# Sliding-window attention before a GeGLU layer: one 256-query score product for key block 2 in place of two 128-query ones, from batch 3 on

One core of one Trainium2 chip. The metric is device time in microseconds (us) of one execution; lower is better.

## The reference

```python
# q, k, v: (8 batches, 8 heads, 576 tokens, 64)
scores = (q @ k^T) / 8 + bias          # bias = -slope(head) * |i - j|
mask   = (i - j >= 0) & (i - j < 128)  # a window of 128 keys, causal
attn   = softmax(where(mask, scores, -1e9))
x      = (attn @ v) as (4608 tokens, 512)
out    = (gelu(x @ w_gate) * (x @ w_val)) @ w_out      # 512 -> 1536 -> 512
```

## The kernel before

The tokens of a batch are shifted by 64 and cut into five blocks of 128, so that the first half of block 0 is padding. With a window of 128, keys of block j meet queries of blocks j and j+1 only. Two heads are worked on as a pair (`i` = 0, 1), each in its own 64 rows of the matmul array; `c` counts the four pairs. Scores are computed with keys on the partitions, so the exponential on ACT and a multiplication by a constant mask and bias on DVE (`emask`: 128 columns for the block's own queries, 128 for the next block's) give the probabilities without a transposition.

The queries come in part 0 (tokens 0 to 319) and part 1 (320 to 575). A score product has one column for each of its queries, and every group of products fills banks of 512 columns of PSUM. The program keeps eight such banks; part 1 of batch 3 takes all eight (four pairs, two banks each):

```python
PART = ((0, 320), (320, 576))
# key block, first and last query of the part that it serves
PIECES = (((0, 0, 192), (1, 64, 320), (2, 192, 320)),
          ((2, 0, 128), (3, 0, 256), (4, 128, 256)))
PCOL = ({0: 64, 1: 256}, {4: 0, 2: 128, 3: 256})

def score(b, c, i, j, qj, n, ps, col):        # keys of block j, n query blocks from qj
    nc.tensor.matmul(out=ps[:, col:col + 128 * n]..., lhsT=blocks(kT, b, i, c, j, 1)...,
                     rhs=blocks(qT, b, i, c, qj, n), start=True, stop=True)

def scores2(b, later=None):                   # the small piece: block 2 with its own queries
    ...
    for c in range(4):
        for i in (0, 1):
            score(b, c, i, 2, 2, 1, ps[i], 128 * c)
    ...                                       # exponential, mask

def scores(b, s, cs, then=None, later=None):
    for c in cs:
        ps = [bank(), bank()]
        for j, qj, n, col in (((0, 0, 2, 0), (1, 1, 2, 256)),
                              ((4, 4, 1, 0), (2, 3, 1, 128), (3, 3, 2, 256)))[s]:
            for i in (0, 1):
                score(b, c, i, j, qj, n, ps[i], col)
    ...                                       # exponential; mask now, or in the list `later`

def sums(b, s):                               # softmax denominators
    for j, a, e in PIECES[s]:                 # key blocks in this order
        for i in (0, 1):
            for c in range(4):
                nc.tensor.matmul(..., lhsT=ones..., rhs=prob(b, s, c, i, j, e - a), ...)
    ...                                       # reciprocal
```

The stages overlap: while the feed-forward layer of token group g runs on TensorE, the scores of batch g+2 and the sums and value products of batch g+1 are put in between. In the loop over g the sums stand here:

```python
        for f in range(7 if g == 0 else 0, NF):
            gate_val(g, f)                    # 8 matmuls of 512 columns, 1.73 us
            ...
            if 2 <= g < B - 1:
                if f == (1 if g == 2 else 0):
                    sums(g + 1, 0)
                if f == (2 if g == 2 else 0):
                    sums(g + 1, 1)
```

So batch 3 (g = 2) has its two sums behind columns 1 and 2 of gate and value; batches 4 to 7 have both behind column 0.

The softmax here doesn't subtract the row's maximum and nothing guards it: scores larger than these inputs give would overflow.

Of the kernel before, what the change touches and what calls it, by code (L numbers as in the profile page):

```python
# [19 lines left out]
          ((2, 0, 128), (3, 0, 256), (4, 128, 256)))  # L20


PCOL = ({0: 64, 1: 256}, {4: 0, 2: 128, 3: 256})


@with_exitstack
def kernel(
# [39 lines left out]
    def bank():  # L67
        ps = psum.tile([128, 512], FP32, name="ps")
        for _ in range(heat.pop()):
            nc.tensor.matmul(out=ps, lhsT=zeros[:, 0:128], rhs=zeros, start=True, stop=True)  # L70
        heat.append(0)
        return ps
# [98 lines left out]
    def blocks(t, b, i, c, j, n):  # L171
        if b < 2:
            return by_pair(t[b])[64 * i:64 * i + 64, c, 128 * j:128 * (j + n)].rearrange(
                "p (n t) -> p n t", n=n)
        return t[b % 2][64 * i:64 * i + 64, j:j + n, c, :]
# [7 lines left out]
    probs, probs2 = {}, {}  # L183

    def score(b, c, i, j, qj, n, ps, col):
        nc.tensor.matmul(  # L186
            out=ps[:, col:col + 128 * n].rearrange("p (n t) -> p n t", n=n),
            lhsT=blocks(kT, b, i, c, j, 1).rearrange("p n t -> p (n t)"),
            rhs=blocks(qT, b, i, c, qj, n),
            start=True, stop=True)  # L190

    def exp(dst, src):
        nc.scalar.activation(out=dst, in_=src, func=AF.Exp, scale=0.125)  # L193

    def mask(dst, m):
        nc.vector.tensor_tensor(out=dst, in0=dst, in1=m, op=ALU.mult)  # L196

    def scores2(b, later=None):

        P = p2_pool.tile([128, 4, 2, 128], BF16, name="P2")  # L200
        probs2[b] = P
        ps = [bank(), bank()]
        for c in range(4):
            for i in (0, 1):
                score(b, c, i, 2, 2, 1, ps[i], 128 * c)
        for i in (0, 1):
            exp(P[:, :, i, :], ps[i].rearrange("p (c n) -> p c n", c=4))
        if later is None:
            for i in (0, 1):
                mask(P[:, :, i, :], emask[:, i:8:2, 0:128])  # L210
        else:
            later.append((P.rearrange("p c i n -> p (c i) n"), emask[:, :, 0:128]))

    def scores(b, s, cs, then=None, later=None):


        pss = []
        for c in cs:
            ps = [bank(), bank()]
            pss.append(ps)  # L220
            for j, qj, n, col in (((0, 0, 2, 0), (1, 1, 2, 256)),
                                  ((4, 4, 1, 0), (2, 3, 1, 128), (3, 3, 2, 256)))[s]:
                for i in (0, 1):
                    score(b, c, i, j, qj, n, ps[i], col)
        if then:
            then()
        for c, ps in zip(cs, pss):
            P = p_pool[s].tile([128, 2, 512], BF16, name="P")
            probs[b, s, c] = P
            for i in (0, 1):  # L230
                exp(P[:, i, :], ps[i])
            args = (P.rearrange("p i (n x) -> p i n x", n=2),
                    emask[:, 2 * c:2 * c + 2, :].unsqueeze(2).to_broadcast((128, 2, 2, 256)))
            if later is None:
                mask(*args)
            else:
                later.append(args)

    def prob(b, s, c, i, j, n):
        if (s, j) == (0, 2):  # L240
            return probs2[b][:, c, i, 0:n]
        return probs[b, s, c][:, i, PCOL[s][j]:PCOL[s][j] + n]

    sumrow, recip = {}, {}

# [12 lines left out]
    def sums0(s):  # L258
        w = WIDE[s]
        ps = bank()  # L260
        todo = []
        for c in range(4):
            for i in (0, 1):
                for j, a, e in ((0, 0, 192), (1, 64, 320)) if s == 0 else PIECES[1]:
                    todo.append((c, i, j, a, e))
        if s == 0:
            todo += [(c, i, 2, 192, 320) for i in (0, 1) for c in range(4)]
        mms = []
        for c, i, j, a, e in todo:
            for x in range(a // w, (e + w - 1) // w):  # L270
                lo, hi = max(a, w * x), min(e, w * x + w)
                g = x if s == 0 else 2 * x + c // 2
                h = 2 * c + i
                mms.append((g, ones4[:, min(j, 1), 32 * h:32 * h + 32] if s == 0 else
                            ones8[:, 32 * (h % 4):32 * (h % 4) + 32],
                            prob(0, s, c, i, j, e - a)[:, lo - a:hi - a], lo - w * x, hi - w * x))
        for n, (g, lhsT, rhs, lo, hi) in enumerate(mms):
            nc.tensor.matmul(
                out=ps[32 * g:32 * g + 32, lo:hi], lhsT=lhsT, rhs=rhs,
                start=all(m[0] != g for m in mms[:n]), stop=all(m[0] != g for m in mms[n + 1:]),  # L280
                skip_group_check=True)
        nc.vector.reciprocal(row(0)[:, PART[s][0]:PART[s][0] + w], ps[:, 0:w])
# [19 lines left out]
    def sums(b, s):  # L302

        ps = bank()
        for j, a, e in PIECES[s]:
            for i in (0, 1):
                for c in range(4):
                    nc.tensor.matmul(  # L308
                        out=ps[32 * c:32 * c + 32, a:e],
                        lhsT=ones[:, min(j, 1), i, :], rhs=prob(b, s, c, i, j, e - a),  # L310
                        start=(i == 0 and j == 2 * s), stop=(i == 1 and j == 2 * s + 2),
                        skip_group_check=True)
        lo, hi = PART[s]
        nc.vector.reciprocal(row(b)[:, lo:hi], ps[:, 0:hi - lo])  # L314
# [27 lines left out]
    def values(b, s, cs=range(4)):  # L342
        lo, hi = PART[s]
        pss = []
        for c in cs:
            ps = bank()
            pss.append(ps)
            for j, a, e in PIECES[s]:
                for i in (0, 1):
                    h = 2 * c + i  # L350
                    nc.tensor.matmul(  # L351
                        out=ps[64 * i:64 * i + 64, a:e],
                        lhsT=vb[b % 2][:, j, 64 * h:64 * h + 64],
                        rhs=prob(b, s, c, i, j, e - a),
                        start=(j == 2 * s), stop=(j == 2 * s + 2), skip_group_check=True)
        for c, ps in zip(cs, pss):
            nc.vector.tensor_tensor(  # L357
                out=xT[:, c, b * S + lo:b * S + hi], in0=ps[:, 0:hi - lo],
                in1=recip[b][:, c, lo:hi], op=ALU.mult)
# [126 lines left out]
    first((0, 1))  # L486
    keep_busy(5)
    scores(0, 0, (0, 1), lambda: (keep_busy(2), first((2,)), first((3,))))
    keep_busy(1)
    scores(0, 0, (2, 3))  # L490
    scores2(0)
    keep_busy(4)
    rest((0, 1))
    rest((2, 3))
    keep_busy(3)
    sums0(0)
    masks, tails = [], []
    scores(0, 1, (0,), None, masks)
    keep_busy(2)
    spread0(0, (act, dve, act, dve))  # L500
# [56 lines left out]
    def flush():  # L557
        for args in masks:
            mask(*args)
        masks.clear()  # L560

    RUN = {"s2": scores2, "s": scores, "sum": sums, "spread": spread_pe, "pv": values,
           "masks": flush, "transposes": transposes_dma, "last": out_last}

# [72 lines left out]
```

## Time and profile before

| | |
|---|---|
| median of the first 3 runs | 358.26 us (358.25 to 358.6) |
| TensorE (PE) busy | 350.5 us, 98% |
| PE's share of the chain that ended last | 89% |
| VectorE (DVE), ScalarE (ACT) busy | 53%, 52% |
| PE's waits, all of the run | 2.9 us, none listed after 100 us |

The prediction below shows the lines and reads them. The early part of a run, loads above all, varies from run to run. So I use the chain in order of time (start, length, what, count), which is the work that led to the last instruction, followed back step by step. From it I take a stretch that begins with the first gate product after batch 3's scores and ends at the start of the last output products. In the kernel before:

```profile
107.69 3.61 PE ps L370 x16
111.30 0.61 PE ps L308 x24
111.91 1.83 PE ps L370 x8
113.74 0.56 PE ps L308 x24
...
351.13 2.63 PE ps L407 x24
```

The stretch is 351.13-107.69 = 243.44 us. The two x24 groups are batch 3's sums of part 0 and part 1.

### The profile page before, as it was taken

The numbers are of one execution on the slowest core, as the hardware profiler recorded it, in microseconds if no ns is written. First come the engines' busy times: TensorE is split into PE (matmuls) and PEld (weight loads), VectorE is DVE, ScalarE is ACT, GpSimd is POOL, SyncE is SP. The second block draws the span as 40 slices with busy tenths as digits, with TensorE's granted clock in tenths as the row PEclk, the third lists the DMA queues.
The fourth block names the chain that finished last, engine by engine and source line by source line (L and its number), as shares of the span: only waits on it lengthen the run. The fifth ranks groups of instructions, "written<-read, shape, count | busy, mean of one in ns | idle before, by whom it ended". The sixth has DMA issues, their size and how long they took to land.

```text
span 357.3 us, 7072 instructions
## 1 busy us (share of the span) xinstructions
PE 350.5 (98%) x2855; PEld 175.0 (49%) x2855; DVE 188.4 (53%) x327; ACT 185.8 (52%) x342; POOL 103.3 (29%) x137
## 2 busy tenths in 40 slices
PE   8999999999999999999999999999999999999996
PEld 3568555444454445445454545445444444444443
DVE  5677469434888646656546554745474403403320
ACT  5874496536878366632973287337833133313322
POOL 8843569600940094002910192004000000000000
PEclk9999999999999999999999999999999999999999
DMA  8999999999999199683998499759205020011002
GB/s 93 177 195 197 203 146 200 147 157 167 134 155 180 39 176 177 120 171 61 145 187 173 90 131 203 139 128 93 85 11 132 26 94 1 2 60 57 2 29 88
DMA packets 145888, 42.62 MB, mean 119 GB/s; under 512 B 131608, under 2 KB 138776, under 8 KB 145856
## 3 DMA queue, kind: packets, MB, share of 16 engines
q0 software_dynamic: 106624, 18.88, 69.7%
q1 hardware_dynamic: 36432, 17.31, 21.7%
q10 hardware_dynamic: 2800, 5.99, 7.7%
q8 instruction: 22, 0.36, 0.4%
q14 instruction: 10, 0.08, 0.1%
HBM read 43.65 MB, written 9.53 MB: 149 GB/s over the span
## 4 chain that ended last, share of the span: by engine, by line
PE 89%; DVE 3%; DMA 3%; POOL 3%; issue 1%; ACT 0%; POOLq 0%; ACTq 0%; DVEq 0%
PE ps L370 52%; PE ps L393 25%; PE ps L351 4%; PE ps L186 4%; DMA wv<-in_moe_w_val_dram 3%; PE ps L308 2%; DVE P L196 1%; DVE r L314 1%; PE ps L407 1%; POOL vb L99 1%; POOL vb L123 0%; POOL wg L133 0%; PE ps L334 0%; POOL ks L123 0%; DVE kT L157 0%
## 5 line engine op out<-in xcount | busy, mean ns | idle before, releaser
L377 DVE TENSOR_TENSOR hT<-ps,gelu 128x512 bf16<-128x512 f32 (+2 forms) x115 | 74.3, 654 | 107.6 <-PE ps L370 92.6
L376 ACT ACTIVATE gelu<-ps 128x512 bf16<-128x512 f32 (+2 forms) x115 | 65.1, 571 | 116.1 <-PE ps L370 114.9
L370 PE MATMUL ps<-xT,wg 128*128 128x512 bf16 (+2 forms) x460 | 112.3, 366 | 0.1
L370 PE MATMUL ps<-xT,wv 128*128 128x512 bf16 (+2 forms) x460 | 112.1, 366 | 0.1
L393 PE MATMUL ps<-wo,hT 128*128 128x512 bf16 x420 | 95.8, 380 | 0.0
L193 ACT ACTIVATE P<-ps 128x512 bf16<-128x512 f32 x144 | 73.1, 631 | 7.6 <-PE ps L186 7.5
L370 PEld LDWEIGHTS <-wv 128*128 128x128 bf16 x460 | 44.6, 98 | 49.1 <-DMA wv<-in_moe_w_val_dram 0.4
L370 PEld LDWEIGHTS <-wg 128*128 128x128 bf16 x460 | 43.2, 98 | 47.1 <-issue 0.3
L196 DVE TENSOR_TENSOR P<-P,emask 128x1024 bf16<-128x1024 bf16 (+1 forms) x79 | 48.8, 640 | 30.9 <-ACT P L193 30.5
L393 PEld LDWEIGHTS <-hT 128*128 128x128 bf16 x420 | 38.9, 98 | 47.7 <-issue 3.6
L99 POOL DMA_DIRECT2D vb<-in_v_dram x40 | 33.9, 879 | 12.9 <-DMA ks<-in_k_dram 5.3
L398 ACT COPY osb<-ps 128x512 f32<-128x512 f32 x31 | 18.7, 602 | 31.2 <-PE ps L393 31.2
L590 POOL COPY mark<-hT 1x2 bf16<-1x2 bf16 x4 | 0.7, 174 | 97.5 <-DVE hT L377 97.5
L357 DVE TENSOR_TENSOR xT<-ps,rb 128x320 bf16<-128x320 f32 (+1 forms) x64 | 24.6, 445 | 7.3 <-DMA rb<-rd 6.1
L314 DVE RECIPROCAL r<-ps 128x320 f32<-128x320 f32 (+1 forms) x14 | 26.8, 1935 | 1.3 <-PE ps L308 1.3
L99 POOL DMA_DIRECT2D qs<-in_q_dram x30 | 25.2, 862 | 7.1 <-DMA wo<-in_moe_w_out_dram 5.1
L99 POOL DMA_DIRECT2D ks<-in_k_dram x30 | 25.4, 889 | 0.7 <-DMA qs<-in_q_dram 0.6
L186 PE MATMUL ps<-qT,kT 64*128 64x256 bf16 (+1 forms) x384 | 22.1, 244 | 1.3 <-DVE kT L157 0.6
L186 PEld LDWEIGHTS <-kT 64*128 64x128 bf16 x384 | 13.4, 94 | 13.3 <-issue 9.6
L351 PE MATMUL ps<-P,vb 128*64 128x128 bf16 (+2 forms) x384 | 18.1, 243 | 0.0
L351 PEld LDWEIGHTS <-vb 128*64 128x64 bf16 x384 | 14.7, 110 | 5.2 <-issue 4.8
L70 PE MATMUL ps<-zeros 128*128 128x512 bf16 x27 | 9.2, 468 | 1.2 <-DVE zeros L418 1.2
(65 smaller groups left out, 116.1 us busy)
## 6 DMA issues: line engine op xcount, KB each, us to landing
out_dram<-osb SPq DMA_DIRECT2D x35, 256.0 KB, 3.4
rb<-rd ACTq DMA_DIRECT2D x10, 576.0 KB, 7.5
vb<-in_v_dram POOLq DMA_DIRECT2D x32, 128.0 KB, 6.7
qs<-in_q_dram POOLq DMA_DIRECT2D x24, 128.0 KB, 5.3
ks<-in_k_dram POOLq DMA_DIRECT2D x24, 128.0 KB, 6.5
wo<-in_moe_w_out_dram POOLq DMA_DIRECT2D x2, 768.0 KB, 17.5
wg<-in_moe_w_gate_dram POOLq DMA_DIRECT2D x2, 384.0 KB, 10.8
wv<-in_moe_w_val_dram POOLq DMA_DIRECT2D x2, 384.0 KB, 11.8
```

Source lines behind the costliest of these rows:

```text
L99: nc.gpsimd.dma_start(out=t[lo:128, j, :].rearrange("p (h d) -> p h d", h=H), in_=src[b][:, 128 * j - 64 + lo:128 * j + 64, :].rearrange(" ...
L186: nc.tensor.matmul(out=ps[:, col:col + 128 * n].rearrange("p (n t) -> p n t", n=n), lhsT=blocks(kT, b, i, c, j, 1).rearrange("p n t -> p ( ...
L193: nc.scalar.activation(out=dst, in_=src, func=AF.Exp, scale=0.125)
L196: nc.vector.tensor_tensor(out=dst, in0=dst, in1=m, op=ALU.mult)
L314: nc.vector.reciprocal(row(b)[:, lo:hi], ps[:, 0:hi - lo])
L351: nc.tensor.matmul(out=ps[64 * i:64 * i + 64, a:e], lhsT=vb[b % 2][:, j, 64 * h:64 * h + 64], rhs=prob(b, s, c, i, j, e - a), start=(j == ...
L357: nc.vector.tensor_tensor(out=xT[:, c, b * S + lo:b * S + hi], in0=ps[:, 0:hi - lo], in1=recip[b][:, c, lo:hi], op=ALU.mult)
L370: nc.tensor.matmul(out=ps[:, 0:hi - lo], lhsT=w[:, c, 128 * f:128 * (f + 1)], rhs=xT[:, c, t0 + lo:t0 + hi], start=(c == 0), stop=(c == 3))
L376: nc.scalar.activation(out=gl[:, 0:hi - lo], in_=pg[:, 0:hi - lo], func=AF.Gelu)
L377: nc.vector.tensor_tensor(out=hid[g][:, f, lo:hi], in0=pv[:, 0:hi - lo], in1=gl[:, 0:hi - lo], op=ALU.mult)
L393: nc.tensor.matmul(out=po, lhsT=hid[g][:, f, 128 * t:128 * (t + 1)], rhs=wo[:, f, :], start=(f == 0), stop=(f == NF - 1))
L398: (nc.vector.tensor_copy if g < 2 and t < 2 else nc.scalar.copy)(out=osb, in_=po)
```

## The change

Key block 2 is multiplied twice for each head before: with query block 2 in the small piece (for part 0) and with query block 3 in part 1. The change makes one product of both in part 1, for batches 3 to 7, and puts block 4, which has only its own queries, into the small piece. The intent is one matmul and one weight load less for each head of these batches; exponentials and masks keep their number.

```diff
-PCOL = ({0: 64, 1: 256}, {4: 0, 2: 128, 3: 256})
+SCORES = ((((0, 0, 2, 0), (1, 1, 2, 256)), ((4, 4, 1, 0), (2, 3, 1, 128), (3, 3, 2, 256))),
+          (((0, 0, 2, 0), (1, 1, 2, 256)), ((2, 2, 2, 0), (3, 3, 2, 256))))
+OWN = (2, 4)
+
+PCOL = ({(0, 0): (0, 64), (0, 1): (0, 256), (0, 2): (2, 0),
+         (1, 4): (1, 0), (1, 2): (1, 128), (1, 3): (1, 256)},
+        {(0, 0): (0, 64), (0, 1): (0, 256), (0, 2): (1, 0),
+         (1, 4): (2, 0), (1, 2): (1, 128), (1, 3): (1, 256)})
@@ scores2
+        j = OWN[b > 2]
-                score(b, c, i, 2, 2, 1, ps[i], 128 * c)
+                score(b, c, i, j, j, 1, ps[i], 128 * c)
@@ scores
-            for j, qj, n, col in (((0, 0, 2, 0), (1, 1, 2, 256)),
-                                  ((4, 4, 1, 0), (2, 3, 1, 128), (3, 3, 2, 256)))[s]:
+            for j, qj, n, col in SCORES[b > 2][s]:
@@ prob
-        if (s, j) == (0, 2):
+        piece, col = PCOL[b > 2][s, j]
+        if piece == 2:
             return probs2[b][:, c, i, 0:n]
-        return probs[b, s, c][:, i, PCOL[s][j]:PCOL[s][j] + n]
+        return probs[b, piece, c][:, i, col:col + n]
```

## The prediction

> **What bounds the kernel now.** I read the views from coarse to fine. The page first: busy shares, and the chain of work that ended last.
>
> ```profile
> span 357.3 us, 7072 instructions
> PE 350.5 (98%) x2855; PEld 175.0 (49%) x2855; DVE 188.4 (53%) x327; ACT 185.8 (52%) x342; POOL 103.3 (29%) x137
> ...
> PE 89%; DVE 3%; DMA 3%; POOL 3%; issue 1%; ACT 0%; POOLq 0%; ACTq 0%; DVEq 0%
> ```
>
> TensorE (PE) is busy for 98% of the span and makes 89% of the chain; no other engine gets beyond 53%. A busy share can hide waits, so next the list of what PE waited for, in all of the run:
>
> ```profile
> PE ps L70 <- DVE zeros L418: 1.2, 1, 1.2
> PE ps L186 <- DVE kT L157: 0.6, 2, 0.4
> PE ps L308 <- DVE P L196: 0.4, 1, 0.4
> PE ps L186 <- DVE rb L340: 0.3, 1, 0.3
> ```
>
> With the two of 0.2 us that follow, this is 2.9 us, and the same list limited to the time after 100 us is empty. The chain adds one short wait that this list does not count, at 107.0 us, where PE needs a bank of PSUM that an exponential still reads. The changed code concerns batches 3 to 7, which begin near 98 us. So in the changed stretch PE works without a gap, and the change can gain only as much as it shortens PE's own stream of work, and can lose only as much as it opens a new wait on PE. Work taken off any other engine is worth nothing there.
>
> What the stream costs is read from the chain in order of time (start, us, what). One steady batch, 6, is scored in the stage from 206.84 us; the first two lines below are the same view for batch 4:
>
> ```profile
> 133.41 0.54 PE ps L186 x8
> ...
> 139.10 0.55 PE ps L186 x12
> ...
> 206.84 0.77 PE ps L186 x16
> 207.61 3.99 PE ps L393 x18
> 211.60 0.76 PE ps L186 x14
> 212.37 3.99 PE ps L393 x18
> 216.36 0.77 PE ps L186 x18
> 217.12 2.70 PE ps L393 x12
> 219.82 1.73 PE ps L370 x8
> 221.55 1.05 PE ps L308 x48
> ```
>
> L186 is the score product, L393 the output product, L370 gate and value, L308 the row sums. From the code the score groups are mixes of narrow products (128 queries) and wide ones (256 queries): x8 is 8 wide; x12 is 8 narrow and 4 wide; x16 is 8 and 8; x14 is 4 narrow and 10 wide; x18 is 12 narrow and 6 wide. They are the quantity on which the whole prediction turns, and they can be solved for: with a for a narrow product, b for a wide one, and t for entering and leaving the group, 8b+t=0.54, 8a+8b+t=0.77, 8a+4b+t=0.55. So 8a=0.23 and a=29 ns; 4b=0.22 and b=55 ns; t=0.10 us. The other two groups check it: x14 gives 0.115+0.55+0.10=0.765 (shown 0.76), x18 gives 0.345+0.33+0.10=0.775 (shown 0.77). The heads of a pair lie in two halves of the array and run side by side, so a pair costs 58 ns narrow and 110 ns wide. Eighteen instructions take as long as fourteen, because both groups have 24 units of 128 columns (12+2x6 and 4+2x10): PE pays for columns, hardly for instructions.
>
> **What the Trainium skill says.** "TensorE: Matmul & The Clock Gate", section "Wait — 56ns, not 53.3ns?", has matmuls start N columns / 2.4 GHz plus about 2.5 ns apart when warm: 55.8 ns for 128 columns, 109.2 ns for 256 (worked out from its formula). My 58 and 110 ns for a pair agree. "Part 3: Packing small matmuls — row/col tiling" of that page says that matmuls in different row groups run concurrently; eight wide ones in 0.54 us, 68 ns each with all overhead, are possible only so. Its section "Back-to-back issue gap" gives some 81 ns per matmul for a stream of weight loads and 128-column matmuls. If that held, removing instructions would pay; the trace does not agree, at 29 ns a product with a weight load of its own each. "Perfetto Trace Analysis", "Tensor Engine Instruction (MATMUL, LD_WEIGHTS)", says that the end of a matmul in a trace is estimated from its size and not observed. That is why I do not take the durations of these rows as costs:
>
> ```profile
> L186 PE MATMUL ps<-qT,kT 64*128 64x256 bf16 x192 | 18.3, 270 | 1.0 <-DVE kT L157 0.6 <-DVE rb L340 0.3
> L186 PE MATMUL ps<-qT,kT 64*128 64x128 bf16 x192 | 11.7, 218 | 0.3 <-DVE xT L357 0.2
> ```
>
> **The change, part by part.** Before, key block 2 is multiplied twice for each head: with query block 2 in the small piece (part 0), and with query block 3 in part 1. Block 4 is a narrow product in part 1. After, for batches 3 to 7, block 2 is one wide product in part 1 and block 4 is the small piece. For each head three narrow products become one narrow and one wide.
>
> *PE's scores.* Removed: 8 heads x 5 batches = 40 matmuls and 40 weight loads. The columns stay. Each removal is worth 2a-b = 2x29-55 = 3 ns; directly from x14 against x18 it is (8a-4b)/4, between 0 and 2.5 ns, as the two groups differ by at most 0.01 us. The skill's formula gives 2x55.8-109.2=2.4 ns for a pair, 1.2 ns a product. I take 0 to 2.5 ns. Batch 3's second part gains nothing: its eight banks are all that PSUM has, and PE then waits at 107.0 to 107.7 us for ACT to empty the first, whatever PE saves. So 32 x 0 to 2.5 ns = 0 to 0.08 us.
>
> *Weight loads.* 40 x 94 ns = 3.8 us less of busy PEld, but PEld is busy for 49% and runs beside the matmuls: nothing on the path.
>
> *ACT and DVE.* Exponentials and masks keep number and shape: the small piece is 2 of 512 columns, each pair of heads 2 of 512. No change, nor in PSUM banks, sums or value products, which only read from other places. Transfers are the same.
>
> *The moved dependence.* This is the part that could hurt. Part 0's sums and values now read block 2 from part 1's tile, which is masked last. Sums of part 0 come first in the code, with block 2 as the last 8 of their 24 matmuls. In the stages for batches 4 to 7 both parts' sums stand together (x48, 1.05 us), so the first need of part 1's tile moves only from matmul 25 to matmul 17, about 0.12 us earlier. For batch 5 (the stage 37 us earlier than the one above) the last mask begins at 182.78 us and lasts 0.69, so ends at 183.47; the sums start at 184.30. For batch 4 the mask ends at 145.97+0.69=146.66, the sums start at 147.12. The slack is 0.8 and 0.5 us before the first sum and some 0.45 us more at the 17th: no wait. Batch 3 differs, as its sums are split: part 0 behind gate-and-value column 1, part 1 behind column 2, two microseconds later.
>
> ```profile
> 111.10 0.69 DVE L196 TENSOR_TENSOR P<-P,emask 128x1024 bf16<-128x1024 bf16 x1
> ...
> 111.23 0.68 PE L308 MATMUL ps<-P,ones 128*32 128x192 bf16 x24
> ...
> 111.84 0.61 PE L370 MATMUL ps<-xT,wg 128*128 128x512 bf16 x2
> ```
>
> Above is the timeline there: DVE on the last mask of batch 3 until 111.79 us, PE beginning part 0's sums at 111.23. Before, these need none of that mask. After, block 2's products reach the fourth head pair at about 111.70 (the last narrow sums of this group are seen to start from 111.68), and must wait for 111.79 plus the 0.05 us that lie between a DVE end and PE's start elsewhere in the chain: 111.84. Then come that product, four more and the switch to the next group. PE loses 0.14 us, I allow 0.1 to 0.25, and nothing takes it back, as PE has no gap later. Batch 3's part 1 sums then wait for nothing.
>
> *Sum.* -0.04 (0 to -0.08) + 0.15 (0.1 to 0.25) = about +0.1 us. On 358.26 this makes 358.35 us.
>
> **Rivals.** (1) *The matmul has a fixed price.* With the 218 ns of the row above for 40 matmuls, two side by side, the gain is 40x218/2=4.4 us, 353.9 us (1.2%). For it speaks only that row's duration; against it, x18 and x14 in equal time. (2) *Weight loads bound the score groups.* Two narrow products need two loads where a wide one needs one. At 94 ns each, bare, the gain is 3.8 us, 354.5 us. But 18 loads at 94 ns are 1.69 us and the whole group takes 0.77: they overlap among themselves and with the matmuls. A small remainder of this is in a, and so already counted. (3) *The new wait is longer.* If part 0's sums stood still for the whole mask from the first matmul (a wait put on the group's first instruction), batch 3 would lose 111.84-111.23=0.6 us and batches 4 to 7 still nothing: 358.8 us. If the slack in those four stages were also used up, for instance by a later exponential, some 0.3 us each would join: near 360 us. Against it: ACT's and DVE's work ahead of these sums is the same, and PE's arrival moves by 0.02 us at most. (4) *The start of the exponentials moves.* A bank with two products completes a little sooner than one with three; ACT is behind in these stages, so nothing follows.
>
> **Range and chances.** The mechanism can give -0.1 to +0.6 us; the three times before spread over 0.35 us. So 357.8 to 358.9 us. A 2% change is 7.2 us, more than rivals 1 and 2 would give and far more than any wait I find: same 0.985, faster 0.005, slower 0.01.
>
> **What would show it.** In the changed kernel's chain, the score groups of batches 5 to 7 read x16, x12, x12 for 0.77, 0.76, 0.76 us (8 wide and 4 wide; 12 wide), with at most 0.02 us less; PE has 40 matmuls fewer, 2815; PEld is 3.8 us less busy; PE's wait list has a new line near 111.7 us, L308 on the mask L196, of 0.1 to 0.25 us; no wait after it. I am wrong if x12 takes under 0.65 us (then instructions cost more than columns), if the new wait is over 0.3 us, or if PE waits on masks in the later stages.

## The result

| | before | after |
|---|---|---|
| median, the runs of the comparison | 358.43 us (358.25 to 358.71, 4 runs) | 358.47 us (358.4 to 358.51, 4 runs) |
| ratio, 95% interval | | 1.0 (0.9983 to 1.0018) |
| span of the profiled run | 357.3 us | 356.7 us |
| stretch from 107 us to the last output products | 243.44 us | 243.62 us |

A ratio is the mean time of one kernel's fast runs over that of the other's of the same rounds, so it is not quite the ratio of the medians in the table. The time is the same. The profiled spans differ by 0.6 us in the changed kernel's favour, but that is no gain: its gate products of that stretch start 0.74 us earlier, and the stretch itself is 0.18 us longer. In the fourteen profiles that start falls anywhere from 106.80 to 107.96 us, without relation to the edit. The stretch leaves out batch 3's own scores, with 8 of the 40 removed products, but they gained nothing either: from the first weight load of batch 3's part 1 to the first gate product behind it the timeline has 1.25 us before (106.44 to 107.69) and 1.24 after (105.71 to 106.95).

The page of the changed kernel:

```profile
span 356.7 us, 6992 instructions
PE 350.1 (98%) x2815; PEld 174.5 (49%) x2815; DVE 188.4 (53%) x327; ACT 185.7 (52%) x342; POOL 103.6 (29%) x137
```

The 40 matmuls and 40 weight loads are gone, and PE is as busy as before. The chain in order of time (L379, L317, L194, L402, L416 are the lines that were L370, L308, L186, L393, L407):

```profile
106.95 3.61 PE ps L379 x16
110.57 0.82 PE ps L317 x24
111.38 1.83 PE ps L379 x8
...
206.30 0.77 PE ps L194 x16
207.06 3.99 PE ps L402 x18
211.06 0.76 PE ps L194 x12
211.82 3.99 PE ps L402 x18
215.81 0.76 PE ps L194 x12
216.57 2.70 PE ps L402 x12
219.26 1.73 PE ps L379 x8
220.99 1.05 PE ps L317 x48
...
350.57 2.63 PE ps L416 x24
```

Batch 6's score groups went from x16, x14, x18 in 0.77, 0.76, 0.77 us to x16, x12, x12 in 0.77, 0.76, 0.76: eight instructions fewer, the same time. Only one group got longer: batch 3's first sums, 0.82 against 0.61 us. The timeline from 110.4 to 111.35 us shows what happens in it (start, length, engine, line, operation):

```profile
109.73 1.32 DVE L204 TENSOR_TENSOR P<-P,emask 128x1024 bf16<-128x1024 bf16 x2
...
110.50 0.39 PEld L317 LDWEIGHTS <-ones 128*32 128x32 bf16 x20 [0.42 <-DVE P L204]
110.50 0.89 PE L317 MATMUL ps<-P,ones 128*32 128x192 bf16 x24
...
111.11 0.10 PEld L317 LDWEIGHTS <-ones 128*32 128x32 bf16 x4 [0.22 <-issue]
```

DVE works on the last two masks of batch 3 until 109.73+1.32 = 111.05 us. The weight loads of the sums stop after the 20th, stand for 0.22 us and go on at 111.11; the row of PE's matmuls, whose lengths are modelled, shows no break at all. A narrow window takes the last five sums out of that row; here it is for the kernel before (window 111.85:111.86) and for the changed one (111.30:111.31):

```profile
111.63 0.28 PE L308 MATMUL ps<-P,ones 128*32 128x128 bf16 x5
111.11 0.27 PE L317 MATMUL ps<-P,ones 128*32 128x128 bf16 x5
```

They begin 3.94 us after the start of the stretch before (111.63-107.69) and 4.16 us after it now (111.11-106.95). The first of those five, the 20th of 24, is the one that needs the last mask. After that PE has no gap in the chain.

### The profile page after: what moved, and what is told of

It reads as the page before. It is cut to its first block, busy times and chain, and to the rows that moved or that the text cites. A ratio compares the mean times of both kernels' runs of the same rounds, so it can differ in the third digit from the quotient of the medians.

```text
span 356.7 us, 6992 instructions
## 1 busy us (share of the span) xinstructions
PE 350.1 (98%) x2815; PEld 174.5 (49%) x2815; DVE 188.4 (53%) x327; ACT 185.7 (52%) x342; POOL 103.6 (29%) x137
## 4 chain that ended last, share of the span: by engine, by line
PE 94%; DVE 4%; issue 0%; ACT 0%; DVEq 0%; ACTq 0%
PE ps L379 53%; PE ps L402 25%; PE ps L360 4%; PE ps L194 4%; PE ps L78 2%; PE ps L317 2%; DVE P L204 1%; DVE r L323 1%; PE ps L155 1%; PE ps L416 1%; DVE kT L165 1%; PE ps L301 1%; PE ps L287 0%; PE ps L343 0%; DVE xT L366 0%
## 5 line engine op out<-in xcount | busy, mean ns | idle before, releaser
L379 PE MATMUL ps<-xT,wg 128*128 128x512 bf16 (+2 forms) x460 | 112.3, 366 | 0.1
L379 PE MATMUL ps<-xT,wv 128*128 128x512 bf16 (+2 forms) x460 | 112.1, 366 | 0.0
L402 PE MATMUL ps<-wo,hT 128*128 128x512 bf16 x420 | 95.8, 380 | 0.0
L379 PEld LDWEIGHTS <-wv 128*128 128x128 bf16 x460 | 44.7, 98 | 48.7
L379 PEld LDWEIGHTS <-wg 128*128 128x128 bf16 x460 | 43.3, 98 | 47.1 <-issue 0.4
L402 PEld LDWEIGHTS <-hT 128*128 128x128 bf16 x420 | 38.9, 98 | 48.1 <-issue 4.0
L407 ACT COPY osb<-ps 128x512 f32<-128x512 f32 x31 | 18.6, 602 | 31.2 <-PE ps L402 31.2
L194 PE MATMUL ps<-qT,kT 64*128 64x256 bf16 (+1 forms) x344 | 22.0, 254 | 1.3 <-DVE kT L165 0.6
L194 PEld LDWEIGHTS <-kT 64*128 64x128 bf16 x344 | 12.7, 94 | 13.5 <-issue 9.6
```

The costliest lines, as they stand in the source:

```text
L194: nc.tensor.matmul(out=ps[:, col:col + 128 * n].rearrange("p (n t) -> p n t", n=n), lhsT=blocks(kT, b, i, c, j, 1).rearrange("p n t -> p ( ...
L379: nc.tensor.matmul(out=ps[:, 0:hi - lo], lhsT=w[:, c, 128 * f:128 * (f + 1)], rhs=xT[:, c, t0 + lo:t0 + hi], start=(c == 0), stop=(c == 3))
L402: nc.tensor.matmul(out=po, lhsT=hid[g][:, f, 128 * t:128 * (t + 1)], rhs=wo[:, f, :], start=(f == 0), stop=(f == NF - 1))
L407: (nc.vector.tensor_copy if g < 2 and t < 2 else nc.scalar.copy)(out=osb, in_=po)
```

## The experiments

Twelve runs were made, of ten further kernels and two repeats, all with correct results. They use 5 or 3 rounds; because most effects here are below 0.3 us, the verdict is read from the stretch of the trace wherever the clock cannot tell.

| run | start, end of the stretch, us | stretch | against after |
|---|---|---|---|
| before | 107.69, 351.13 | 243.44 | -0.18 |
| after | 106.95, 350.57 | 243.62 | |
| after_2 | 106.85, 350.47 | 243.62 | 0.00 |
| from_b4 | 107.38, 350.79 | 243.41 | -0.21 |
| early_before | 107.31, 350.76 | 243.45 | -0.17 |
| early_after | 106.91, 352.25 | 245.34 | +1.72 |
| split | 107.45, 351.22 | 243.77 | +0.15 |
| extra_64 | 107.61, 353.08 | 245.47 | +1.85 |
| extra_128 | 106.86, 354.05 | 247.19 | +3.57 |
| extra_256 | 107.96, 358.56 | 250.60 | +6.98 |
| merged | 107.08, 350.27 | 243.19 | -0.43 |
| merged_2 | 107.17, 350.36 | 243.19 | -0.43 |
| merged_before | 106.86, 350.08 | 243.22 | -0.40 |
| trim | 106.80, 349.60 | 242.80 | -0.82 |

For early_after the chain does not pass through the first gate product, so its start is read from the timeline. The kernels that ran twice (after and after_2, merged and merged_2) repeat to 0.01 us in this measure, while single times by the clock in their second runs range from 358.4 to 359.06 us and from 357.98 to 360.48 us.

### Is the wait in batch 3 the cost?

**from_b4** puts the old arrangement back for batch 3 only.

```diff
-        j = OWN[b > 2]
+        j = OWN[b > 3]
-            for j, qj, n, col in SCORES[b > 2][s]:
+            for j, qj, n, col in SCORES[b > 3][s]:
-        piece, col = PCOL[b > 2][s, j]
+        piece, col = PCOL[b > 3][s, j]
```

> The change from batch 4 on instead of batch 3, so that part 0's sums of batch 3 need nothing of part 1's tile again. My theory (PE pays for columns; the only real cost is one wait in batch 3): against the changed kernel, 0.2 us less; in the trace the first sums group of batch 3 falls back from 0.82 to 0.61 us in the chain and the later score groups still read 0.77, 0.76, 0.76 for x16, x12, x12. Against the kernel before: 0 to 0.08 us less (32 products removed at 0 to 2.5 ns). Rival (a fixed price for each instruction, hidden in the changed kernel by something other than this wait): 32 products at 218/2 ns would show here as 3.5 us less than before.

By the clock nothing can be told: 358.62 us (358.41 to 359.69), ratio to before 1.0005 (0.9992 to 1.0017). In the trace the stretch is 0.21 us shorter than the changed kernel's and 0.03 us shorter than that of before, and the chain has the short group again:

```profile
110.99 0.61 PE ps L317 x24
```

So the wait is batch 3's, it is 0.21 us, and the 32 products removed in batches 4 to 7 are worth 0.03 us together, 1 ns each. That is only three times the 0.01 us to which repeats agree; but merged_before and merged, below, where no wait comes in, also differ by 0.03 us in the stretch. The 3.5 us of the fixed price do not exist, hidden or not.

**early_after and early_before** move batch 3's first sums one column up, where a wait on the last mask would be 1.73 us longer.

```diff
-                if f == (1 if g == 2 else 0):
+                if f == 0:
                     sums(g + 1, 0)
```

> The changed kernel with batch 3's part 0 sums one gate-and-value column earlier, behind column 0. If these sums now hang on the last mask of part 1, PE meets them 1.73 us earlier and stands still until that mask is done: a wait of about 1.73 + 0.2 = 1.9 us, 360.2 us in all, 1.7 us over the changed kernel. If the 0.21 us longer sums group in the changed kernel is something else (other reads, a busier memory), the time stays within 0.3 us of the changed kernel.

> The same one line in the kernel before, where part 0's sums need only masks that end near 109.3 us; PE arrives near 109.4 us. My theory: within 0.2 us of the kernel before. Rival (the early place itself costs, by its bank of PSUM or by the reciprocal standing in front of DVE's work): also about 1.7 us slower, and then the run above shows nothing of the moved dependence.

The changed kernel with it takes 360.62 us (360.2 to 362.65), ratio to before 1.0075 (1.0051 to 1.0099), and its stretch is 1.72 us longer. The kernel before with it takes 358.82 us (358.7 to 359.2), ratio 1.0008 (0.9995 to 1.0021), its stretch unchanged at 243.45 us. The place costs nothing; the dependence costs. PE's timeline in early_after (PE's rows alone):

```profile
108.73 0.71 PE L317 MATMUL ps<-P,ones 128*32 128x192 bf16 x17
109.83 0.22 PE L317 MATMUL ps<-P,ones 128*32 128x128 bf16 x1 [0.39 <-DVE P L204]
110.43 0.22 PE L317 MATMUL ps<-P,ones 128*32 128x128 bf16 x1 [0.39 <-DVE P L204]
111.07 0.27 PE L317 MATMUL ps<-P,ones 128*32 128x128 bf16 x5 [0.42 <-DVE P L204]
```

Here the same thing is seen enlarged: the group runs 17 products, then advances one product for each mask as DVE finishes it, and the last five start at 111.07 us, as in the changed kernel. It also shows a limit of the view. The idle times in brackets sum to 1.2 us, but the wait by the stretches is 0.21+1.72 = 1.93 us. Each row's modelled length of some 0.22 to 0.27 us runs into the gap behind it and hides that much of it.

### What does a score product cost?

Three kernels add 128 products to the changed one: each wide score product of batches 4 to 7 is followed by another one with the same weights into the same place, of 256, 128 or 64 columns. The result does not change. Each added product has a weight load of its own: the page counts 2943 loads against 2815.

```diff
                 for i in (0, 1):
                     score(b, c, i, j, qj, n, ps[i], col)
+                if b > 3 and n == 2:
+                    for i in (0, 1):
+                        extra(b, c, i, j, qj, 256, ps[i], col)     # or 128, or 64
```

> The changed kernel with every wide score product of batches 4 to 7 done a second time into the same place (same result): 128 more products of 256 columns. Columns theory: 55 ns each, 7.0 us more. Fixed price of an instruction (218/2 ns): 14 us, the same as in extra_128 and extra_64. Weight loads bare (94 ns): 12 us, again the same in all three.

> The same 128 more products, but of 128 columns each. Columns theory: 29 ns each, 3.7 us more, half of extra_256. Either rival: the same as extra_256.

> The same 128 more products of 64 columns each. Columns theory without a floor: [...]15 ns each, 1.9 us more. If something in each instruction takes its own time (the weight load, the issue), there is a floor, and this run is near extra_128 (3 to 3.7 us): then the narrow product of 128 columns stands just at the floor and removing one is worth little only by that accident.

The stretch grows by 6.98, 3.57 and 1.85 us, so one product costs 54.5, 27.9 and 14.5 ns. By the clock the medians are 366.26, 362.63 and 361.02 us, the ratios to before 1.0204 (1.0185 to 1.0223), 1.0104 (1.0081 to 1.0127) and 1.0066 (1.004 to 1.0093). From 64 to 256 columns the price rises by 40.0 ns for 192 columns, 0.208 ns each; what is left without columns is 14.5-64x0.208 = 1.2 ns. So these products show no floor down to 64 columns, which I had left open. Both rivals, which want the same price for all three, are out.

**split** makes each wide product of batches 4 to 7 two narrow ones: 128 more instructions, no more columns.

```diff
+                if b > 3 and n == 2:
+                    for m in (0, 1):
+                        for i in (0, 1):
+                            score(b, c, i, j, qj + m, 1, ps[i], col + 128 * m)
+                    continue
                 for i in (0, 1):
                     score(b, c, i, j, qj, n, ps[i], col)
```

> The change turned around and enlarged: every wide score product of batches 4 to 7 as two narrow ones, so 128 more instructions and weight loads, no more columns. Columns theory: 128 x (0 to 2.5 ns) = 0 to 0.3 us more than the changed kernel. Fixed price rival: 128 x 218/2 = 14 us more; bare weight loads: 12 us more; a price of the instruction that is hidden only where the changed kernel's removals were: several us.

Its time is 359.44 us (358.58 to 361.1), ratio 1.0019 (0.999 to 1.0048), which leaves the clock undecided between nothing and some tenths of a microsecond, but rules out 12 us. The stretch says +0.15 us, 1.2 ns for each added instruction, the same as the remainder above. Batch 6's three score groups in its chain:

```profile
206.87 0.78 PE ps L194 x24
...
211.64 0.78 PE ps L194 x24
...
216.41 0.78 PE ps L194 x24
```

Twice as many products as in the changed kernel's x12 take 0.02 us more.

### A version without the wait, and one that takes away columns

**merged** leaves the changed kernel's scores and puts both sums of batch 3 behind column 2; **merged_before** does the same to the kernel before.

```diff
-                if f == (1 if g == 2 else 0):
+                if f == (2 if g == 2 else 0):
                     sums(g + 1, 0)
```

> The changed kernel with both parts' sums of batch 3 together behind column 2. The wait must go (the last mask is done some 1.7 us before), and one entry into a group of small products goes too: from x24 0.61 and x24 0.56 in the chain to one x48 of 1.05 us, 0.12 us. So 0.2 + 0.12 = 0.3 us less than the changed kernel, 0.15 less than the kernel before. Rival (the wait is taken over by the reciprocals, which start later, and through the gather by the rest): the time is that of the changed kernel or more.

> The merged kernel again, on the same chip as the trimmed one: in the trace 243.2 us from the first gate product of the stage after batch 3's scores to the last output product, 0.25 less than the kernel before; by the clock some 0.3 us less than before, near what can be told apart.

> The same merging in the kernel before. It has no wait to take away, only one entry into a group of small products: 0.12 us less in the same stretch of the trace, 243.3 against 243.44. If it gains 0.3 like the merged changed kernel, then the merging and not the end of the wait was the gain there.

The merged changed kernel is at 358.26 us (358.02 to 358.38), ratio 0.999 (0.9978 to 1.0002), in its first run, and at 358.16 us (357.98 to 360.48), ratio 1.0001 (0.998 to 1.0021), in the second: not told apart from before by the clock. In the stretch it gains 0.43 us on the changed kernel. I had expected 0.3. (The last mask ends 1.2 us before these sums start, not 1.7; either way PE meets no wait.) merged_before gives the reason: with no wait to lose, it gains 0.22 us (243.44 to 243.22) and not 0.12; by the clock 358.17 us (358.02 to 358.71), ratio 0.9991 (0.9979 to 1.0003). So the merging alone is worth 0.22 and the end of the wait the other 0.21. Its chain shows both halves of the 0.22:

```profile
106.86 5.34 PE ps L370 x24
112.20 1.05 PE ps L308 x48
```

The sums take 1.05 us against 0.61+0.56 = 1.17 before, and the 24 gate and value products around them 5.34 against 3.61+1.83 = 5.44. I had counted the first half only.

**after_2** is the changed kernel once more, beside these.

> The changed kernel again beside these: 243.6 us in that stretch, 0.18 more than the kernel before, and by the clock within 0.3 us of it.

It came out at 358.62 us (358.4 to 359.06) with before at 358.64, ratio 1.0001 (0.9989 to 1.0013), and 243.62 us for the stretch.

**trim** follows from the price list: only columns count, so the 64 padded queries of block 0 are worth removing even at the cost of an instruction. A first form, in which the exponential still read the 64 columns that nothing had written, was rejected by the memory check and never ran; this one reads 448 columns and masks in two instructions. It is built on merged.

```diff
+                    if j == 0 and b > 2:                       # 64 queries of block 0
+                        score(b, c, i, 0, 0, 1, ps[i], 0, 64)  # skip the first 64
+                    else:
                         score(b, c, i, j, qj, n, ps[i], col)
+                for i in (0, 1):
+                    if j == 0 and b > 2:                       # 128 queries of block 1
+                        score(b, c, i, 0, 1, 1, ps[i], 128)
...
-                exp(P[:, i, :], ps[i])
+                exp(P[:, i, lo:], ps[i][:, lo:])               # lo = 64 in part 0, else 0
```

> The version built on what the runs so far gave: sums of batch 3 merged behind column 2, and from batch 3 on the product of key block 0 without the 64 padded queries: one product of 256 columns becomes one of 64 and one of 128 (the exponential reads 448 columns, the mask is two instructions). The three runs with extra products gave 14.5, 27.9 and 54.5 ns for 64, 128 and 256 columns in the trace, so each of 40 gains 54.5-14.5-27.9 = 12.1 ns though the instructions become more: 0.5 us less than the merged kernel, 0.39 of it after 107 us. Rival (more instructions cost, or the doubled masks hold the sums up): no gain or a loss.

Its median is 357.67 us (357.53 to 358.81), ratio to before 0.9982 (0.9968 to 0.9995): 0.2% faster, an interval that stays below 1, though far from 2%. The stretch is 242.80 us, 0.39 less than merged, as worked out. The shorter exponentials also took 2.1 us off ACT's busy time (185.7 to 183.6), but in merged PE had no wait in this stretch that a faster ACT could have shortened. It is the fastest of the kernels here, with 40 matmuls more than the changed one.

## Why the prediction was right

- **PE bounds the changed stretch without a gap.** Shown, but for the one new wait. Each edit that lengthened or shortened PE's stream changed the stretch by about what had been worked out for it: 6.98, 3.57 and 1.85 us for 7.0, 3.7 and 1.9, and -0.39 for -0.39.
- **PE pays for columns: 29 and 55 ns, and 0 to 2.5 ns for a removed instruction.** Shown, with 27.9 and 54.5 ns by extra_128 and extra_256, and 1.2 ns by split. The 32 removals outside batch 3 gave 0.03 us against 0.04 predicted.
- **Weight loads lie beside.** Right for the time, wrong for the view: I wrote that PEld would be busy 3.8 us less, and it is 0.5 us less (175.0 to 174.5). I multiplied 40 by the 94 ns of a row, but loads overlap each other, and the page's busy time counts overlapped time once: in the kernel before, the 14 loads of batch 6's second score group stand within 0.61 us, and all 384 score loads of 94 ns make 13.4 us, 35 ns each.
- **One new wait, in batch 3, none in batches 4 to 7.** Shown by from_b4 and by the pair early_after and early_before. Its size is 0.21 us against 0.15 predicted (0.1 to 0.25). The mask's end and the delay to PE were right (111.11-111.05 = 0.06 us). PE's arrival was misread: I took 111.70 us for it, close to a merged row that begins at 111.68, but that row leaves out the 20th sum, which in the kernel before starts at 111.63 (the x5 row above). From there to my 111.84 are the 0.21 us.
- **The sum.** +0.1 us predicted; +0.18 in the stretch; by the clock 358.47 against 358.43 in the same comparison, and 358.62 against 358.64 in a second one. Rival 3's 0.6 us did not come: the wait stands at the 20th of 24 sums and not at the first.
- **What the number alone would show.** Little: my range of 357.8 to 358.9 us also holds the kernel before, so a change that did nothing at all would have landed in it. That the account is right rests on the stretch and the experiments, not on the clock.
- **The sign to look for was wrong.** I wrote that PE's wait list would have a new line. It has none; its only line of this kind is the one that was there before, from a wait at 58.53 us, long before batch 3's sums:

```profile
PE ps L317 <- DVE P L204: 0.4, 1, 0.4
```

The gap of 0.2 us is covered by the modelled length of the product in front of it (0.22 to 0.27 us in the rows of early_after). The group's length in the chain showed the wait, and so did the break in the weight loads of the timeline.

## What to carry to other kernels

In a kernel like this one, where TensorE is full and its products have 64 to 256 columns, count the columns that it streams, not the instructions: joining two 128-column products into one of 256 saved 1 ns, while leaving out 64 useless columns saved 12 ns even though it took one more instruction. When a product moves to another tile, ask when the last part of that tile is ready and who meets it first; an order in which everything was ready can contain one place where it now is not. Where effects are a tenth of a per cent, compare a stretch of the trace between two fixed instructions, not spans, whose starts vary by more than the effect.

## What the Trainium skill lacked or had wrong

- "TensorE: Matmul & The Clock Gate", section "Back-to-back issue gap": some 81 ns per matmul for a stream of weight loads and 128-column matmuls. Here such a product with its own weight load costs 27.9 ns, 56 ns for the pair of row halves, which is the page's other formula (N/2.4 + 2.5 ns, which it calls isolated); at 64 columns 14.5 ns, 29 ns for the pair. For 512 columns the section gives some 131 ns; the gate and value products here, each with a weight load of its own, take 216 ns (1.73 us for 8).
- The same page, "Part 3: Packing small matmuls — row/col tiling", gives concurrent starts for row tiles, but no price for a long stream of pairs. The runs give one: each product of a pair costs 0.208 ns for a column and 1.2 ns beside.
- "TensorEngine Tiling (Array Packing)", section "Key Properties", says that changing the tiling mode drains the engine, without a number. One group of 128x32 sums less between 128x128 products saved 0.22 us (merged_before). The runs do not show that the drain is the cause; the weight loads also pause there.
- "Perfetto Trace Analysis", section "Tensor Engine Instruction (MATMUL, LD_WEIGHTS)", says that matmul ends are estimated, but not what follows for waits: a wait of 0.21 us on PE was listed as none, and one of 1.93 us as 1.2.
